# Attention and two dense layers on one core: transposes that write tokens in order, the softmax guard on ScalarE, low parts of weights on either engine, and a new issue order

## The chip, the core and the metric

The kernel runs on one NeuronCore of a Trainium2 chip. The metric is device time in microseconds (us): 627.39 us, the median of three runs (627.38 to 627.73). TensorE (PE) multiplies matrices into PSUM banks; VectorE (DVE), ScalarE (ACT) and GpSimd (POOL) work on tiles; SyncE (SP) issues the DMAs. Each engine works off its own queue in order and waits on semaphores for the others.

## The reference

```python
def _attn_ref(q, k, v):                       # (2, 8, 768, 64) each
    k_sum = k.reshape(B, H, nb, 32, D).max(axis=3)
    v_sum = v.reshape(B, H, nb, 32, D).mean(axis=3)
    scores_l = scale * q @ k.T                # kept where |i - j| < 16
    scores_s = scale * q @ k_sum.T + np.log(32)
    scores_all = np.concatenate([scores_l_m, scores_s], axis=-1)
    a = np.exp(scores_all - max)
    a = a / (np.sum(a, axis=-1, keepdims=True) + 1e-09)
    return a @ np.concatenate([v, v_sum], axis=2)

x = attn_out.transpose(0, 2, 1, 3).reshape(1536, 512)
h = x @ w_in;  x = (h * np.clip(h + 3, 0, 6) / 6) @ w_out        # 512 -> 2048 -> 512
h = x @ w_in2; return (h * sigmoid(h)) @ w_out2                  # the same sizes
```

## The kernel before

The tokens of a batch are cut into 12 units of 64 queries, 24 units in all. A unit `u` sees 96 keys around it and 24 block keys, 120 slots for each of 4 pairs of heads. Its steps are `keys` (key window gathered, POOL or DVE), `scores` (PE), `masked` (DVE: add the mask, take the maximum), `exps` (ACT: exponential with the row sum), `guard` (DVE: 1e-9 added to a 128x4 tile of sums), `inverse` (DVE), `normal` (POOL or DVE: 128x480 multiply), `turn` (PE transposes), `turned` (copy out of PSUM), `mix` (PE), `mixed_hi` and `mixed_lo` (the result as two fp32r parts, a high one and what is left).

Before that, `load` fetches two neighbouring tokens into one partition, `par` separates even from odd tokens, and `tr` transposes 128x128 pieces (four per call, 24 calls) into a PSUM bank: even tokens fill one 128-column stretch, odd ones the next. `k_copy`, `k_max` and `q_copy` put the tokens back in order as they read the bank. `q_copy` fills, for each pair of heads, the two diagonal blocks of the query tile (64 partitions each, one instruction for each, 48 instructions in all).

The dense layers take every product as high x high + high x low + low x high. A half weight `h` (64 of them, 128x1024 words of 32 bits holding 512 wide numbers) is fetched and converted: `conv_mag` (ACT), `conv_low`, `conv_clamp`, `conv_join`, `conv_sign` (DVE), `conv_hi` (ACT, or DVE where starred), `conv_lo` (GpSimd). Step `i` then has `hidden` (PE, 12 products), `act` (ACT), `gate` (DVE), `gate_hi`, `gate_lo`, `project` (PE, 12 products). The first 32 steps work on 256 tokens, the other 80 on 512. The first `hidden` needs the four first units' `mixed_lo`, and its weights.

The order of everything is the text `ORDER`, a list of 1920 steps; each engine's queue is that list with the other engines' steps left out. A star puts a step on DVE where its function asks for it (`copier`, `keys`, `normal`, `gate_lo`, `q_copy`). `conv_lo` does not ask: the 31 stars on it do nothing, and all 64 run on GpSimd. Buffers come from rings: 7, later 8 PSUM banks, 3 buffers of fetched words, 2 of `bits`, 1 of `mag`, 3 of gated results.

The lines that the text names: L481 par, L495 tr, L503 k_copy, L510 k_max, L526 and L528 q_copy on DVE and ACT, L535 v_pair, L573 v_put, L589 and L590 keys, L612 masked, L626 exps, L637 guard, L641 inverse, L646 normal, L654 turn, L659 turned, L666 mix, L688 and L692 mixed_hi and mixed_lo, L406 conv_mag, L411 conv_low, L418 conv_clamp, L424 conv_join, L431 conv_sign, L442 conv_hi, L445 conv_lo, L708 hidden, L728 and L732 gate, L736 gate_hi, L742 gate_lo, L764 and L767 project.

Of the kernel before, what the change touches and what calls it, by code (L numbers as in the profile page):

```python
# [87 lines left out]
k_max 0 2 0, keys 3*, keys 2*, tr q 0 1 0, k_copy 0 2 1, scores 3, q_copy 0 1 1 1, k_copy 0 2 0*, keys 1,
load v 0 0, conv_low 0, q_copy 0 1 1 0, keys 0, masked 3, conv_mag 0, scores 1, scores 2, conv_clamp 0,
conv_low 1, scores 0, conv_join 0, rouse 5, v_sums 0 0, masked 2, q_copy 0 1 0 0, keys 7, keys 4,  # L90
load q 0 2, masked 0, exps 3, keys 6, q_copy 0 1 0 1, tr q 0 2 0, tr q 0 2 1, conv_mag 1, conv_clamp 1,
guard 3, fetch 2, exps 2, rouse 0, inverse 3, keys 5, masked 1, scores 6, normal 3, exps 0, guard 2, turn 3,
inverse 2, conv_join 1, scores 7, conv_sign 0, conv_hi 0*, exps 1, load v 0 2, conv_mag 2, load v 0 1,
rouse 7, conv_sign 1, guard 0, conv_lo 0*, keys 10, inverse 0, rouse 3, rouse 4, q_copy 0 2 0 0, normal 2,
masked 7, rouse 2, q_copy 0 2 1 1, v_add 0 0, v_sums 0 2, v_sums 0 1, conv_hi 1, guard 1, scores 5,
conv_clamp 2, q_copy 0 2 1 0, turn 2, conv_low 2, fetch 3, load v 1 0, warm 0, normal 0, exps 7, v_add 0 1,
inverse 1, load_v 2, load_v 1, warm 1, q_copy 0 2 0 1, v_add 0 2, rouse 1, normal 1*, turn 1, load_v 3,
v_rows 0, turn 0, conv_join 2, masked 6, fetch 4, conv_mag 3, guard 7, conv_lo 1, turned 3, load_v 0,
turned 2, conv_sign 2, conv_low 3, masked 5, v_pair 1 0, turned 1, v_put 0 2, inverse 7, keys 9*, exps 5,
scores 4, load v 1 1, v_sums 1 0, conv_clamp 3, keys 8*, warm 2, conv_join 3, normal 7, guard 5, mix 2,  # L100
inverse 5, scores 9, v_put 0 0, mixed_hi 2, v_put 0 1, v_put 0 3, masked 4, conv_hi 2, unstage, normal 5,
conv_sign 3, mix 1, v_add 1 0, turned 0*, turn 5, load k 1 0, scores 8, conv_lo 2, exps 4, mixed_hi 1,
load_v 5, mixed_lo 2, v_pair 1 1, guard 4, mixed_lo 1, conv_hi 3, conv_mag 4, mix 3, inverse 4, turned 5,
mix 0, v_sums 1 1, turn 7, tr k 1 0 0, mixed_hi 0, mixed_hi 3*, conv_low 4, conv_clamp 4, conv_join 4,
keys 11, mixed_lo 0, exps 6, fetch 5, mixed_lo 3, turned 7, tr k 1 0 1, masked 9, guard 6, conv_lo 3,
fetch 6, inverse 6, load_v 4, conv_low 5, mix 5, conv_sign 4, hidden 1 0, normal 4, v_add 1 1, conv_mag 5,
k_max 1 0 1, exps 9, hidden 0 0, hidden 1 1, load k 1 1, conv_clamp 5, guard 9, conv_hi 4, conv_join 5,
hidden 0 1, act 0, turn 4, load_v 6, turned 4, inverse 9, fetch 7, mixed_hi 5, conv_mag 6, normal 6,
load_v 7, masked 8, gate 0, scores 10, mixed_lo 5, act 1, conv_lo 4, gate 1, conv_low 6, conv_clamp 6,
mix 4, scores 11, k_copy 1 0 1, conv_join 6, conv_sign 6, mixed_hi 4, gate_hi 0, turn 6, k_copy 1 0 0,  # L110
turned 6, hidden 2 0, tr k 1 1 1, tr k 1 1 0, conv_sign 5, conv_hi 6, k_copy 1 1 0, mixed_lo 4, gate_hi 1,
masked 10, mix 6, k_max 1 0 0, conv_lo 6, gate_lo 0, hidden 2 1, load k 1 2, mixed_hi 6, conv_low 7,
load v 1 2, conv_hi 5, fetch 8, mix 7, hidden 3 0, gate_lo 1, load_v 11, mixed_hi 7, conv_mag 7, fetch 9,
mixed_lo 7, k_max 1 1 0, k_copy 1 1 1, hidden 3 1, project 0 0, act 2, act 3, tr k 1 2 0, mixed_lo 6,
masked 11, gate 2, hidden 4 0, conv_lo 5, project 1 0, gate_hi 2, v_pair 1 2, gate 3, exps 10, conv_clamp 7,
hidden 4 1, conv_join 7, conv_low 8, k_max 1 1 1, gate_lo 2, k_copy 1 2 0, conv_sign 7, conv_mag 8,
# [828 lines left out]
```

## Time and profile before

| what | value |
|---|---|
| median of three runs | 627.39 us |
| the profiled execution's own time | 628.69 us |
| its span, first to last instruction | 626.9 us |
| PE busy | 605.1 us (97%) |
| DVE / ACT / POOL busy | 411.0 / 250.4 / 137.5 us |
| mean granted TensorE clock | 0.997 |

The profiled execution took 1.3 us more than the median of the runs; 1.8 us of it lie outside the span. PE's 97% leaves 21.8 us idle. Where they lie is read from a table by stage, below: most of them are in the first 47 us, in which the attention's first units and the first weights are made ready by DVE, ACT and POOL, and the first `hidden` starts at 47.76 us.

### The profile page before, as it was taken

What the parts mean: (1) busy time and instruction counts of PE and PEld (TensorE: products, weight loads), DVE (VectorE), ACT (ScalarE), POOL (GpSimd) and SP (SyncE); (2) the same over time, 40 slices, a digit from 0 to 9 for tenths busy, and PEclk for the clock granted to TensorE, in tenths of its full rate; (3) what the DMA queues carried; (4) which work ended last, traced back from release to release, by engine and by line L of the source; (5) the groups of instructions that cost most, each with busy time, mean ns of one, the idle gap of its engine ahead of it and who ended that gap; (6) DMA issues with size and microseconds to landing.
All of it is one profiled execution on the core that took longest, in us unless ns stands there. A gap on an engine that the chain in (4) does not pass through costs nothing.

```text
span 626.9 us, 9556 instructions
## 1 busy us (share of the span) xinstructions
PE 605.1 (97%) x3590; PEld 518.8 (83%) x3590; DVE 411.0 (66%) x920; ACT 250.4 (40%) x603; POOL 137.5 (22%) x131
## 2 busy tenths in 40 slices
...
GB/s 252 266 226 191 182 173 145 15 51 11 64 58 101 100 102 67 101 122 47 67 68 35 100 101 67 68 67 68 2 66 34 43 25 2 0 68 1 67 1 67
DMA packets 69054, 51.61 MB, mean 82 GB/s; under 512 B 36368, under 2 KB 63504, under 8 KB 69008
## 3 DMA queue, kind: packets, MB, share of 16 engines
...
q14 instruction: 18, 0.15, 0.1%
...
## 4 chain that ended last, share of the span: by engine, by line
PE 76%; DVE 17%; ACT 3%; issue 2%; DMA 1%; POOL 0%; SPq 0%; ACTq 0%; DVEq 0%; POOLq 0%
PE bank L708 35%; PE bank L767 20%; PE bank L764 16%; DVE bits L424 2%; DVE bits L431 2%; DVE bits L411 2%; DVE mag L418 2%; PE bank L597 1%; PE bank L666 1%; DVE gw L742 1%; DVE stat L637 1%; DVE prob L612 1%; PE bank L654 1%; DMA stage<-in_k_dram 1%; PE bank L495 1%
## 5 line engine op out<-in xcount | busy, mean ns | idle before, releaser
L708 PE MATMUL bank<-x,w 128*128 128x512 f32 (+1 forms) x912 | 185.0, 349 | 1.1 <-DVE rn L728 1.0
L708 PEld LDWEIGHTS bank<-x,w 128*128 128x128 f32 x912 | 149.0, 191 | 23.5 <-DVE rn L728 2.0
L445 POOL TENSOR_TENSOR w<-bits,w 128x512 fp32r<-128x512 f32 x48 | 70.5, 1473 | 241.6 <-ACT w L442 139.9
L767 PE MATMUL bank<-w,gw 128*128 128x512 f32 (+1 forms) x456 | 103.6, 378 | 0.1
L767 PEld LDWEIGHTS bank<-w,gw 128*128 128x128 f32 x456 | 82.5, 188 | 16.6 <-DVE gw L742 0.5
L722 ACT ACTIVATE rw<-bank 128x512 f32<-128x512 f32 x48 | 28.3, 597 | 131.9 <-PE bank L708 98.6
L742 DVE TENSOR_TENSOR gw<-rw,gw 128x512 fp32r<-128x512 f32 x80 | 59.4, 749 | 32.0 <-ACT gw L736 30.3
L732 DVE TENSOR_TENSOR rw<-bank,rw 128x512 f32<-128x512 f32 x48 | 32.8, 687 | 63.3 <-ACT rw L722 63.0
L708 PE MATMUL bank<-x,we 128*128 128x512 f32 x240 | 59.3, 389 | 0.0
L764 PE MATMUL bank<-gw,w 128*128 128x512 f32 x240 | 58.6, 390 | 0.3 <-DVE gw L742 0.3
L406 ACT ACTIVATE mag<-words 128x512 f32<-128x512 f32 x64 | 43.1, 673 | 36.4 <-DVE bits L424 28.0
L764 PE MATMUL bank<-gn,w 128*128 128x256 f32 x384 | 54.6, 287 | 1.0 <-DVE gn L742 0.5
L764 PEld LDWEIGHTS bank<-gw,w 128*128 128x128 f32 x240 | 44.9, 188 | 10.4 <-DVE gw L742 1.2
L708 PEld LDWEIGHTS bank<-x,we 128*128 128x128 f32 x240 | 45.0, 188 | 9.4
L431 DVE SCALAR_TENSOR_TENSOR bits<-words,bits 128x512 uint32<-128x512 uint32 x64 | 50.7, 795 | 0.6
L736 ACT CAST gw<-rw 128x512 fp32r<-128x512 f32 x43 | 26.7, 621 | 60.2 <-PE bank L767 26.7
L764 PEld LDWEIGHTS bank<-gn,w 128*128 128x128 f32 x384 | 48.7, 191 | 2.0 <-issue 0.8
L424 DVE SCALAR_TENSOR_TENSOR bits<-mag,bits 128x512 uint32<-128x512 uint32 x64 | 49.4, 772 | 1.1
L411 DVE TENSOR_SCALAR bits<-words 128x512 uint32<-128x512 uint32 x64 | 36.7, 573 | 9.2 <-POOL w L445 5.7
L418 DVE TENSOR_SCALAR mag<-mag 128x512 f32<-128x512 f32 x64 | 33.9, 529 | 8.7 <-ACT mag L406 8.5
L445 POOL TENSOR_TENSOR we<-bits,we 128x512 fp32r<-128x512 f32 x16 | 22.2, 1393 | 75.7 <-DVE we L442 45.4
L736 DVE CAST gw<-rw 128x512 fp32r<-128x512 f32 x37 | 16.5, 449 | 33.6 <-PE bank L767 29.4
(105 smaller groups left out, 764.6 us busy)
## 6 DMA issues: line engine op xcount, KB each, us to landing
...
```

The costliest lines, as they stand in the source:

```text
L406: nc.scalar.activation(out=out, in_=low_high(h)[:, 1].bitcast(F32), func=AF.Abs, scale=EXP_SHIFT)
L411: nc.vector.tensor_scalar(out=bitss.take(h, 2), in0=low_high(h)[:, 0], scalar1=2.0**-29, scalar2=7.0, op0=ALU.mult, op1=ALU.min,)
L418: nc.vector.tensor_scalar(out=mag, in0=mag, scalar1=MAG_MIN, scalar2=MAG_MAX, op0=ALU.max, op1=ALU.min)
L424: nc.vector.scalar_tensor_tensor(out=bits, in0=mags.use(h).bitcast(U32), scalar=3, in1=bits, op0=ALU.logical_shift_left, op1=ALU.bitwise_or,)
L431: nc.vector.scalar_tensor_tensor(out=bits, in0=low_high(h)[:, 1], scalar=0x80000000, in1=bits, op0=ALU.bitwise_and, op1=ALU.bitwise_or,)
L445: nc.gpsimd.tensor_tensor(out=w_half(h, 1), in0=bitss.use(h).bitcast(F32), in1=w_half(h, 0).bitcast(F32), op=ALU.subtract,)
L708: nc.tensor.matmul(ps[:, :n], w[:, a, kk * P : (kk + 1) * P], x[:, o // SUB : (o + n) // SUB, b, kk, :], start=(m == 0), stop=(m == last),)
L732: nc.vector.tensor_tensor(out=r[:, :n], in0=ps[:, :n], in1=r[:, :n], op=ALU.mult)
L736: copier("gate_hi", i)(out=gs.take(i, 1)[:, 0, :n], in_=rs.use(i)[:, :n])
L742: eng.tensor_tensor(out=g[:, 1, :n], in0=r[:, :n], in1=g[:, 0, :n].bitcast(F32), op=ALU.subtract)
L764: nc.tensor.matmul(ps[:, o : o + n], lhs, g[:, b, :n], **flags)
L767: nc.tensor.matmul(ps[:, : len(cols)], g[:, a, rows], rhs, **flags)
```

## The change

Five edits are made together. (1) `tr` writes even tokens to even columns and odd ones to odd columns of the bank, so a transpose's output has a stride of two elements, and the readers (`k_copy`, `k_max`, `q_copy`, `mixed`) take tokens in order. (2) `q_copy` works on one head parity `e` for two pairs of heads: one instruction of 64x512 where two of 64x256 stood; 24 instead of 48. (3) `guard` becomes an ACT instruction. (4) `conv_lo` goes to DVE where starred: 37 of 64, 7 of them before the attention's buffers are given up. (5) `ORDER` is another permutation of the same 1920 steps, with other stars.

```diff
 ORDER = """
-table 0, load k 0 1, par k 1 1, load q 0 0, par k 1 0, tr k 0 1 1, par q 0 0, load k 0 0, par q 0 1,
...
+zero, table 0, load k 0 0, par k 0 1, par k 0 0, tr k 0 0 1, tr k 0 0 0, rouse 7, k_max 0 0 1, load k 0 2,
...
@@ -442,7 +441,8 @@
         copier("conv_hi", h)(out=w_half(h, 0), in_=bitss.use(h).bitcast(F32))
 
     def conv_lo(h):
-        nc.gpsimd.tensor_tensor(
+        eng = nc.vector if ("conv_lo", h) in ON_DVE else nc.gpsimd
+        eng.tensor_tensor(
             out=w_half(h, 1), in0=bitss.use(h).bitcast(F32), in1=w_half(h, 0).bitcast(F32),
             op=ALU.subtract,
         )
@@ -488,12 +488,12 @@
         key = (what, b, T)
         raw = raws.use(key) if key in raws.held else parts.use((what + "p", b, T))
         ps = banks.take((what, b, T, half), 2)
+        tokens = ps.rearrange("p (i j r) -> p i r j", i=2, r=2)
         for i in range(2):
             h0 = 2 * (2 * half + i)
             for r in range(2):
-                o = (2 * i + r) * P
                 nc.tensor.transpose(
-                    ps[:, o : o + P], raw[:, r * DM + h0 * D : r * DM + h0 * D + P], ident
+                    tokens[:, i, r], raw[:, r * DM + h0 * D : r * DM + h0 * D + P], ident
                 )
 
     def k_copy(b, T, half):
@@ -501,31 +501,31 @@
         hs = slice(2 * half, 2 * half + 2)
         dst = kT[b][:, hs, PAD + 256 * T : PAD + 256 * (T + 1)]
         copier("k_copy", b, T, half)(
-            out=dst.rearrange("p i (j r) -> p i r j", r=2),
-            in_=ps.rearrange("p (i r j) -> p i r j", i=2, r=2),
+            out=dst, in_=ps.rearrange("p (i t) -> p i t", i=2)
         )
 
     def k_max(b, T, half):
         ps = banks.use(("k", b, T, half))
         nc.vector.tensor_reduce(
             out=kmax[b][:, 2 * half : 2 * half + 2, 8 * T : 8 * (T + 1)],
-            in_=ps.rearrange("p (i r n j) -> p i n r j", i=2, r=2, n=8),
-            axis=AX.XY,
+            in_=ps.rearrange("p (i n t) -> p i n t", i=2, n=8),
+            axis=AX.X,
             op=ALU.max,
         )
 
-    def q_copy(b, T, half, i):
+    def q_copy(b, T, half, e):
         if (b, T) not in qTs.held:
             qTs.take((b, T), 4)
         ps = banks.use(("q", b, T, half))
-        dst = qTs.see((b, T))[:, 2 * half + i].rearrange("p w (e r j) -> p w e r j", e=2, r=2)
-        src = ps[:, 256 * i : 256 * (i + 1)].rearrange("p (r w j) -> p w r j", r=2, w=4)
-        for e in range(2):
-            rows = slice(e * D, e * D + D)
-            if ("q_copy", b, T, half, i) in ON_DVE:
-                nc.vector.tensor_scalar_mul(dst[rows, :, e], src[rows], 1.0 / math.sqrt(D))
-            else:
-                nc.scalar.mul(dst[rows, :, e], src[rows], 1.0 / math.sqrt(D))
+        rows = slice(e * D, e * D + D)
+        dst = qTs.see((b, T))[rows, 2 * half : 2 * half + 2, :, e * QW : e * QW + QW].rearrange(
+            "p i w t -> p (i w) t"
+        )
+        src = ps[rows].rearrange("p (v t) -> p v t", t=QW)
+        if ("q_copy", b, T, half, e) in ON_DVE:
+            nc.vector.tensor_scalar_mul(dst, src, 1.0 / math.sqrt(D))
+        else:
+            nc.scalar.mul(dst, src, 1.0 / math.sqrt(D))
 
     def v_pair(b, T):
 
@@ -634,7 +634,7 @@
 
     def guard(u):
         st = sts.see(u)
-        nc.vector.tensor_scalar_add(st[:, 1], st[:, 1], 1e-9)
+        nc.scalar.activation(out=st[:, 1], in_=st[:, 1], func=AF.Identity, bias=1e-9)
 
     def inverse(u):
         st = sts.use(u)
@@ -674,11 +674,8 @@
     def mixed(u):
         ps = banks.use(("m", u))
         j, o = divmod(u * QW, WIDE)
-        src = ps[:, : NHP * QW].rearrange("p (h r j) -> p h r j", h=NHP, r=2)
-        hi, lo = (
-            x1[j][:, o // SUB, i, :, o % SUB : o % SUB + QW].rearrange("p h (j r) -> p h r j", r=2)
-            for i in range(2)
-        )
+        src = ps[:, : NHP * QW].rearrange("p (h q) -> p h q", h=NHP)
+        hi, lo = (x1[j][:, o // SUB, i, :, o % SUB : o % SUB + QW] for i in range(2))
         return src, hi, lo
 
     def mixed_hi(u):
@@ -842,7 +839,7 @@
     raws = ring(apool, "qkv", 2, [P, 2 * DM])
     gs = ring(apool, "gn", LAG + 1, [P, 2, SUB], F32R)
     rs = ring(apool, "rn", 2, [P, SUB])
-    qTs = ring(apool, "qT", 2, [P, NHP, 4, P])
+    qTs = ring(apool, "qT", 2, [P, NHP, 4, 2 * QW])
     sts = ring(apool, "stat", 4, [P, 3, NHP])
```

Line numbers differ between the two kernels: in the changed one `guard` is still L637, but `hidden` is L705 (L708 before), `mixed_lo` L689 (L692), `mixed_hi` L685 (L688), `conv_join` L423 (L424), `conv_sign` L430 (L431), `conv_clamp` L417 (L418), `conv_low` L410 (L411), `conv_mag` L405 (L406), `conv_hi` L441 (L442), `k_max` L509 (L510).

On DVE, this is what stands before, around the `mixed_lo` (L692) of the first four units, whose results the first `hidden` waits for (`x_0` is the tile of the first tokens, `stat` a unit's sums, `bits` and `mag` weights in conversion):

```order
L555 COPY vsum<-bank_80 128x128
L659 COPY pT_111<-bank_76 120x512
L692 TENSOR_TENSOR x_0_64<-bank_78,x_0_64 128x4x2x32
L637 TENSOR_SCALAR stat_105<-stat_105 128x4
L692 TENSOR_TENSOR x_0_64<-bank_77,x_0_64 128x4x2x32
L641 RECIPROCAL stat_105<-stat_105 128x4
L688 CAST x_0_64<-bank_81 128x4x2x32
L411 TENSOR_SCALAR bits_69<-words_72 128x512
L418 TENSOR_SCALAR mag_68<-mag_68 128x512
L424 SCALAR_TENSOR_TENSOR bits_69<-mag_68,bits_69 128x512
L692 TENSOR_TENSOR x_0_64<-bank_80,x_0_64 128x4x2x32
L692 TENSOR_TENSOR x_0_64<-bank_81,x_0_64 128x4x2x32
```

And on DVE now, at the same place (the `mixed_lo` are L689; L573 is `v_put`, L535 `v_pair`, L445 `conv_lo`):

```order
L423 SCALAR_TENSOR_TENSOR bits_70<-mag_68,bits_70 128x512
L573 COPY early_units<-bank_75 24x512
L430 SCALAR_TENSOR_TENSOR bits_70<-words_72,bits_70 128x512
L689 TENSOR_TENSOR x_0_64<-bank_81,x_0_64 128x4x64
L535 TENSOR_TENSOR qkv_93<-qkv_93 128x8x64
L689 TENSOR_TENSOR x_0_64<-bank_78,x_0_64 128x4x64
L689 TENSOR_TENSOR x_0_64<-bank_79,x_0_64 128x4x64
L689 TENSOR_TENSOR x_0_64<-bank_76,x_0_64 128x4x64
L445 TENSOR_TENSOR w_91<-bits_69,w_91 128x512
L641 RECIPROCAL stat_103<-stat_103 128x4
L417 TENSOR_SCALAR mag_68<-mag_68 128x512
```

No `guard` stands there any more; a `v_put`, a `v_pair` and a `conv_lo` that ran on ACT and POOL do.

On ACT, the first `exps` (L626) and what stands between them before (L528 is `q_copy`, L406 `conv_mag`):

```order
L626 ACTIVATE early_units,stat_102<-early_units,stat_102 128x120 x4
L528 ACTIVATE qT_101<-bank_77 64x4x64 x2
L406 ACTIVATE mag_68<-words_72 128x512
L626 ACTIVATE early_units,stat_103<-early_units,stat_103 128x120 x4
L626 ACTIVATE prob_109,stat_104<-prob_109,stat_104 128x120 x4
L626 ACTIVATE prob_110,stat_105<-prob_110,stat_105 128x120 x4
```

And on ACT now, from the first `exps` on (L637 is `guard`, L441 `conv_hi`):

```order
L626 ACTIVATE early_units,stat_102<-early_units,stat_102 128x120 x4
L637 ACTIVATE stat_102<-stat_102 128x4
L405 ACTIVATE mag_68<-words_73 128x512
L626 ACTIVATE early_units,stat_103<-early_units,stat_103 128x120 x4
L637 ACTIVATE stat_103<-stat_103 128x4
L626 ACTIVATE prob_109,stat_104<-prob_109,stat_104 128x120 x4
L441 CAST w_90<-bits_70 128x512
L637 ACTIVATE stat_104<-stat_104 128x4
L626 ACTIVATE prob_110,stat_105<-prob_110,stat_105 128x120 x4
```

Each unit's `guard` follows its `exps` on the same engine, once with a `conv_hi` between them.

On PE, the first `hidden` (L708) and what precedes it before (L544 is `v_sums`, L654 `turn`, L495 `tr`, L666 `mix`):

```order
L544 MATMUL bank_76<-qkv_94,cst 32x128 x4
L654 MATMUL bank_78<-cst,early_units 120x128 x4
L495 MATMUL bank_77<-cst,qkv_93 128x128 x4
L495 MATMUL bank_74<-cst,qkv_93 128x128 x4
L666 MATMUL bank_80<-pT_112,vwin_114 64x64 x8
L708 MATMUL bank_81<-x_0_64,w_91 128x256 x6
L708 MATMUL bank_78<-x_0_64,w_90 128x256 x6
```

And on PE now (L597 is `scores`, L705 `hidden`):

```order
L666 MATMUL bank_78<-pT_112,vwin_114 64x64 x8
L666 MATMUL bank_76<-early_units 64x64 x8
L654 MATMUL bank_75<-cst,prob_109 120x128 x4
L597 MATMUL bank_81<-kw_107,qT_100 128x120 x4
L654 MATMUL bank_78<-cst,early_units 120x128 x4
L705 MATMUL bank_79<-x_0_64,w_90 128x256 x6
L544 MATMUL bank_76<-qkv_94,cst 32x128 x4
L705 MATMUL bank_75<-x_0_64,w_91 128x256 x6
```

In both queues about the same attention work stands ahead of the first `hidden`: ten `scores`, six `turn`, five `mix` and fourteen `tr` before, twelve, six, four and twelve now.

## Rows read from the trace of the kernel before

**Rows 1.** Table by stage; engine columns are busy us (instructions), then PE's granted clock.
```profile
0.00:47.20 47.20, 31.27 (x326) 26.56 (x328) 38.19 (x132) 38.34 (x117) 24.99 (x39) 1.00 1.04 248
47.20:80.00 32.80, 32.28 (x300) 30.69 (x295) 32.53 (x90) 24.20 (x73) 14.79 (x12) 0.95 0.71 177
80.00:120.00 40.00, 38.18 (x363) 35.84 (x362) 34.17 (x100) 26.92 (x81) 16.85 (x18) 1.00 0.51 130
200.00:300.00 100.00, 99.85 (x440) 82.09 (x439) 80.36 (x132) 39.46 (x69) 23.42 (x18) 1.00 0.30 95
600.00:627.00 27.00, 23.76 (x128) 20.35 (x126) 10.73 (x19) 1.80 (x3) 0.00 (x0) 1.00 0.11 39
```

**Rows 2.** Timeline around the first `hidden`: start us, duration us, engine; idle before it in brackets.
```profile
46.93 0.90 PE L666 MATMUL bank<-pT,vwin 120*64 120x64 f32 x16 [2.49 <-DVE x L692]
...
47.76 4.40 PE L708 MATMUL bank<-x,w 128*128 128x256 f32 x24
```

**Rows 3.** The guard in that timeline, free and beside a POOL instruction.
```profile
47.93 0.16 DVE L637 TENSOR_SCALAR stat<-stat 128x4 f32<-128x4 f32 x1
...
48.23 0.42 DVE L411 TENSOR_SCALAR bits<-words 128x512 uint32<-128x512 uint32 x1
...
50.76 1.55 POOL L445 TENSOR_TENSOR w<-bits,w 128x512 fp32r<-128x512 f32 x1 [1.28 <-ACT w L442]
51.08 1.25 DVE L637 TENSOR_SCALAR stat<-stat 128x4 f32<-128x4 f32 x1
```

**Rows 4.** DVE groups, 0 to 47.2 us: count, busy us, mean ns, idle before.
```profile
L411 DVE TENSOR_SCALAR bits<-words 128x512 uint32<-128x512 uint32 x5 | 4.0, 792 | 0.0
L418 DVE TENSOR_SCALAR mag<-mag 128x512 f32<-128x512 f32 x5 | 3.8, 755 | 0.2 <-ACT mag L406 0.2
L637 DVE TENSOR_SCALAR stat<-stat 128x4 f32<-128x4 f32 x7 | 3.7, 532 | 0.6 <-ACT prob L626 0.6
L526 DVE TENSOR_SCALAR qT<-bank 64x256 f32<-64x256 f32 x2 | 0.8, 418 | 0.0
L503 DVE COPY kT<-bank 128x512 f32<-128x512 f32 x1 | 0.7, 680 | 0.0
L589 DVE COPY kw<-kT 128x384 f32<-128x384 f32 x2 | 0.7, 334 | 0.0
L590 DVE COPY kw<-kmax 128x96 f32<-128x96 f32 x2 | 0.4, 197 | 0.0
```

**Rows 5.** POOL groups, 0 to 47.2 us.
```profile
L445 POOL TENSOR_TENSOR w<-bits,w 128x512 fp32r<-128x512 f32 x4 | 5.7, 1414 | 2.7 <-DVE w L442 2.0 <-ACT w L442 0.7
L646 POOL TENSOR_TENSOR prob<-prob,stat 128x480 f32<-128x480 f32 x3 | 3.4, 1129 | 1.7 <-ACT x L688 1.7
L646 POOL TENSOR_TENSOR early_units<-early_units,stat 128x480 f32<-128x480 f32 x3 | 3.0, 1003 | 3.8 <-DVE stat L641 3.8
L535 POOL TENSOR_TENSOR qkv<-qkv 128x512 f32<-128x512 f32 x2 | 2.7, 1351 | 0.2 <-DMA qkv<-in_v_dram 0.2
```

**Rows 6.** ACT groups over the whole run.
```profile
L720 ACT ACTIVATE rw<-bank 128x512 f32<-128x512 f32 x32 | 18.8, 595 | 39.7 <-PE bank L708 19.8 <-DVE gw L742 19.8
L528 ACT ACTIVATE qT<-bank 64x256 f32<-64x256 f32 x42 | 15.8, 377 | 1.6 <-PE bank L495 0.6 <-DVE qT L526 0.5
L626 ACT ACTIVATION_READ_ACCUMULATOR prob<-prob,stat 128x1 f32 x72 | 13.6, 189 | 0.0
```

**Rows 7.** DVE, a subtraction of the size of `conv_lo`, whole run; then the guard, 0 to 120 us.
```profile
L742 DVE TENSOR_TENSOR gw<-rw,gw 128x512 fp32r<-128x512 f32 x80 | 59.4, 749 | 32.0 <-ACT gw L736 30.3
...
L637 DVE TENSOR_SCALAR stat<-stat 128x4 f32<-128x4 f32 x16 | 8.5, 532 | 0.9 <-ACT prob L626 0.9
```

**Rows 8.** Timeline, 90 to 92 us: a DVE instruction that reads two SBUF tiles.
```profile
90.85 1.15 POOL L646 TENSOR_TENSOR early_units<-early_units,stat 128x480 f32<-128x480 f32 x1
91.08 1.20 DVE L742 TENSOR_TENSOR gn<-rn,gn 128x256 fp32r<-128x256 f32 x1
```

**Rows 9.** PE, the transposes L495 of loaded tiles, whole run.
```profile
L495 PE MATMUL bank<-cst,qkv 128*128 128x128 f32 x64 | 9.5, 275 | 1.5 <-DMA qkv<-in_q_dram 1.5
```

More of the change, by code (lines that the diff above doesn't have):

```diff
@@ L88 @@
[L88 to L116, printed above, removed]
-normal 9, conv_hi 7, act 4, v_sums 1 2, v_add 1 2, exps 11, conv_clamp 8, conv_join 8, conv_sign 8,
@@ L133 @@
-project 9 0, conv_sign 13, mixed_hi 8, q_copy 1 0 0 0, conv_clamp 14, v_put 1 0, conv_join 14, mixed_lo 8,
-project 9 1, load q 1 1, gate 10, gate_hi 10, conv_sign 14, hidden 13 0, gate_lo 10*, scores 13, conv_hi 14,
-inverse 10, normal 11, conv_lo 14, masked 13, hidden 13 1, fetch 18, act 13, gate 13, keys 15, conv_mag 15,
-scores 12, hidden 11 0, conv_low 15, load q 1 2, masked 12, gate_lo 12, turn 11, conv_hi 13, v_put 1 1,
-gate_hi 13*, hidden 11 1, conv_lo 13*, normal 10*, exps 13, gate_lo 13, act 11, conv_clamp 15, guard 13,
@@ L143 @@
-gate_hi 15, mix 10, tr q 1 1 1, fetch 16, keys 17*, scores 14, turn 12, project 13 0, mixed_hi 10*,
-project 13 1, turned 12, masked 14, inverse 15, q_copy 1 1 1 1, tr q 1 2 0, gate_lo 14, mix 13, mixed_lo 10,
-normal 15*, q_copy 1 2 0 0, exps 14, q_copy 1 1 1 0, project 14 0, q_copy 1 2 0 1*, gate_lo 15*,
-hidden 18 0, guard 14, project 14 1, project 15 0, tr q 1 2 1, inverse 14, turn 15, hidden 18 1,
-finish 0 0 0 0, act 18, scores 17, normal 14, gate 18, turned 15, project 15 1, turn 14, keys 16*,
@@ new lines @@
+q_copy 0 2 0 1, conv_low 3, conv_join 3, guard 7, inverse 7, normal 7, scores 9, load_v 0, fetch 4, guard 4,
+v_put 0 3, load_v 3, masked 5, turned 1, conv_mag 4, conv_sign 3, conv_clamp 4, inverse 4, normal 4,
+conv_low 4, scores 11, mix 3, v_put 0 1, scores 10, v_put 0 0, mix 0, masked 6, conv_join 4, exps 5,
+guard 5, turned 2, mixed_hi 0, mixed_hi 3, load_v 1, mix 1, load_v 2, v_put 0 2*, conv_sign 4, mixed_hi 1,
+conv_hi 4, mixed_lo 0, load v 1 1, v_pair 1 1*, mixed_lo 1, mixed_lo 3, conv_hi 3, mix 2, mixed_hi 2,
```

404 lines of the change are left out of this document (219 added, 185 removed).

## The prediction, made before the changed kernel ran

> **What bounds the kernel now.** I read the table by stage first. PE is busy 200 of 200 us in the middle and, from 47.2 us to 120, idle only 32.8-32.28 + 40-38.18 = 2.3 us; in the first 47.2 us it is idle 15.9, and 3.2 us in the last slice, where the last results leave [rows 1]. So the time is PE's work, which no edit shortens, plus those waits. PE's wait before the first products of the dense layers is the one to look at: the `mix` at 46.93 us had waited 2.49 us for DVE's `mixed_lo`, and the first `hidden` follows at 47.76 [rows 2]. DVE is busy 38.2 of these 47.2 us; 5.8 of the rest is the first DMA. ACT has 38.3, its table load included, but DVE is what PE waits for [rows 1, 2]. So the start is DVE's queue up to the fourth `mixed_lo`: what is in it, and how long its instructions are held up.
>
> They are held up. The guard takes 0.16 us at 47.93, yet 1.25 us at 51.08, when a POOL subtraction runs from 50.76 to 52.31; `conv_low` (L411) takes 0.42 us alone [rows 3] and 0.79 on average up to 47.2 us, `conv_clamp` (L418), of the same kind and size, 0.755 [rows 4]. Guards: 7 x (0.53-0.16) = 2.6 us lost. The two conversions: 5 x (0.79-0.42) + 5 x (0.755-0.42) = 3.5 us. The POOL work beside it is 12 large instructions, 14.8 us [rows 5].
>
> **The change, part by part.** *DVE up to the fourth `mixed_lo`.* By the two queues, out go 7 guards, 3.7 us [rows 4], and three small ones, a reciprocal, a `v_add`, a `mixed_hi`, which I put at 0.2, 0.3 and 0.4 us, about the sizes of the smaller rows there (a 128x96 copy 0.2, 64x256 from PSUM 0.42 [rows 4]). In come three `keys` pairs at 0.33+0.20 [rows 4], 1.6 us; one `conv_sign`, one `turned` and one `v_put`, each a 512-wide instruction, at the 0.68 of the 512-wide copy [rows 4], 2.0 us; one `v_pair` at 0.75 [rows 7]; and two `q_copy` of 64x512 where two of 64x256 stood. The trace has no 64x512; it lies between 0.42 and 0.68, and as the width and not the partitions sets the others, I take 0.68: +0.5. In: 4.9 us; out: 4.6. Net +0.3.
>
> *What holds DVE up.* POOL has in its queue, up to the same place, 3 `conv_lo` and 5 `normal`, no `v_pair`: 8 large instructions for 12. If the 3.5 us of the conversions fall in proportion, 3.5 x 8/12 = 2.3: -1.2. The other stretched instructions (joins, signs, copies) I leave. The bounds: if the stalls do not fall at all, 0; and a guard's stall may pass on to the instruction behind it, up to the whole 2.6 us. If instead they all but vanish, -3.5. I take -1.2, the proportional share. The first `hidden` comes 0.3 - 1.2 = -0.9 us earlier.
>
> The start-up itself stays: the first DVE instruction still waits for the first load of k. The query tile now comes fourth in SP's queue, but `scores` need the maxima of all of k anyhow. The mask table is issued behind one more fetch of weights (512 KB; at the 248 GB/s of that stage [rows 1], 2 us later). It is wanted by the first `masked`, which the new order puts behind seven more DVE instructions, so I take 0; without that cover it would cost up to 2 us.
>
> *ACT.* Seven guards come in. The nearest small ACT instruction takes 0.19 us, the next one up 0.38 (64x256) [rows 6]: 1.3 us, at most 2.7. The `q_copy` go from 22 x 0.377 = 8.3 us to 10 x 0.595 = 6.0, taking the 512-wide ACT row [rows 6]. ACT is 1.0 us lighter, between 2.3 lighter and 0.4 heavier. The guard now runs behind its own `exps` with no change of engine, and DVE no longer stands in its queue waiting for it (0.6 us [rows 4]): -0.6.
>
> *Copies and transposes.* On DVE `k_max`, `mixed_hi` and `mixed_lo` read as many elements as before; 0, with the gain of a plain order unknown (0 to -0.5 us in all, as none is much above its like). The 96 transposes write with a stride of two. The trace has none such; 64 of them took 0.148 us each [rows 9]. At one end nothing changes; at the other each takes twice that, 96 x 0.148 = 14 us, of which a third lies in PE's idle time. I take 0, as the number of columns is the same.
>
> *From 47 to 120 us.* Nine guards leave DVE, 8.5-3.7 = 4.8 us [rows 4, 7]; seven `conv_lo` come, 7 x 0.75 = 5.2 us [rows 7], and leave POOL, 7 x 1.41 = 9.9 us of its 31.6 here [rows 1, 5]. With a third of POOL's work gone, DVE is held up less. PE can gain no more than its 2.3 us of idle and the 0.05 x 32.8 = 1.6 us that the granted clock of 0.95 costs [rows 1]. I take -0.5, between -3 and +2.
>
> *After 120 us.* Thirty more `conv_lo` put 22.5 us on DVE, which is busy 80 of 100 us at most there [rows 1], while PE waits 0.15 us in that stretch. I take 0 and keep +1: a `gate` queued behind a `conv_lo` is 0.75 us later, while a step is 24 products of PE.
>
> Sum: -0.9 - 0.6 - 0.5 = -2.0 us. The profiled execution took 628.7 us (a span of 626.9 and 1.8 around it), so it would be 626.7; it stood 1.3 above the median of 627.4, and on that scale the forecast is **625.4 us**, its own range 623.0 to 626.1.
>
> **The rivals.** *A: the stalls only move.* A guard that waits 1.1 us for POOL is gone, but the next DVE instruction that meets the same POOL instruction waits in its place: the 2.6 us come back, and -2.0 becomes +0.6: 628.0 us, within what a measurement of this kernel can tell from no change (0.2%, 1.25 us). For it: the subtraction L742 took 1.20 us beside a POOL multiply [rows 8], against a mean of 0.75 for one twice as wide [rows 7], so `conv_lo` and `v_pair`, which read two tiles as it does, can be held up as the guard was. Against it: the instructions that follow a guard in these queues are often `masked` and `mixed_lo`, which read PSUM. The Trainium skill (SBUF — State Buffer, Who interferes with whom) says that a DVE instruction with two SBUF inputs contends with a GpSimd instruction that reads SBUF, and that the one issued second waits until the first ends; by that rule moving `conv_lo` to DVE does not leave the contest, it enters it from the other side. The rows just named agree.
>
> *B: slower, DVE late at the first `hidden`.* The place is the same queue. If the shorter POOL list frees nothing and the guards' 2.6 us pass on in full, and DVE waits as often as before, it is 0.3 + 2.6 = +2.9 there, and with nothing won afterwards 630.3 us. It decides once DVE needs over 38.2 + 1.25 = 39.4 us of work up to the fourth `mixed_lo`. For it: net of stalls the new queue is longer. Against: 8 POOL instructions instead of 12.
>
> *C: more is won.* ACT lighter and POOL lighter end cross-waits too: the conversions' 3.5 us go entirely instead of by 1.2, and 1 us more of the later idle: -2.0 - 2.3 - 1.0 = -5.3, 622.1 us. Against: DVE's list is not shorter.
>
> *D: the strided transposes cost.* Two thirds of the 14 us bound: 636 us. Nothing speaks for it but that no row shows such a write.
>
> **How the numbers follow.** Forecast 0.42, C 0.08, A 0.28, B 0.19, D 0.03. Faster by over 0.2% 0.50, within 0.2% 0.28, slower 0.22. The range reaches to C's price below and short of B's above: 622.3 to 629.5 us.
>
> **What would show it.** The first `hidden` at 45.5 to 47.3 us; DVE busy at most 37.7 us up to it; `conv_low` and `conv_clamp` at a mean under 0.7 us there; no DVE row for the guard, and an ACT row of about 0.2 us; PE idle under 2.3 us from there to 120 us, and still under 1 us in 200 to 400. It is wrong if the first `hidden` is no earlier than 47.8 us, if `conv_clamp` and the joins are stretched as much as before (A or B), or if the transposes' mean is above 0.15 us (D).

## The result and the profile after

The changed kernel took 619.94 us (median of 4 runs, 619.72 to 620.51) against 627.43 (627.38 to 627.73): a ratio of 0.9881, 95% interval 0.9864 to 0.9898, or 7.5 us less. The forecast of 625.4 us had the right sign, but the result lies 2.4 us below the range that it gave (622.3 to 629.5). The profiled execution took 620.01 us, a span of 618.2, against 628.69 and 626.9; that of before stood 1.3 us above its median, so the traces differ by 8.7 us where the medians differ by 7.5.

The stage table of the changed kernel (stretch and its length in us; busy us and instructions of PE, weight loads, DVE, ACT and POOL; granted clock, DMA share, GB/s), to be laid beside [rows 1]:

```profile
0.00:47.20 47.20, 35.23 (x329) 32.02 (x330) 36.94 (x143) 35.67 (x109) 20.55 (x32) 0.96 0.93 231
47.20:80.00 32.80, 32.80 (x338) 31.17 (x337) 31.17 (x88) 25.42 (x83) 17.81 (x17) 1.00 0.99 229
80.00:120.00 40.00, 40.00 (x397) 38.49 (x396) 31.49 (x103) 27.15 (x84) 9.71 (x14) 1.00 0.38 99
200.00:300.00 100.00, 100.00 (x443) 82.76 (x442) 77.63 (x137) 36.36 (x64) 9.33 (x6) 1.00 0.29 92
600.00:619.00 19.00, 15.09 (x81) 12.88 (x79) 7.48 (x13) 1.11 (x2) 0.00 (x0) 1.00 0.15 55
```

PE's idle time fell from 15.9 to 12.0 us in the first stage and from 2.3 us to nothing between 47.2 and 120 us. In that second stretch (the two rows added) PE did 735 instructions where it had done 663. POOL was busy 27.5 us there for 31.6, and DVE 62.7 for 66.7, though DVE had been given the work. Further on PE's pace is the same: 443 instructions in 100 us for 440.

All that PE still waits for, by the list of its waits (who waited for whom: us in total, times, longest):

```profile
PE bank L495 <- DVE stage L481: 6.8, 2, 5.9
PE bank L563 <- DVE vsum L557: 2.1, 1, 2.1
PE bank L597 <- ACT qT L528: 1.7, 1, 1.7
PE bank L654 <- POOL prob L646: 1.2, 1, 1.2
```

The first is the start-up; the wait for `mixed_lo` of [rows 2] is not in the list any more. The timeline at that place (start, duration, engine):

```profile
44.28 1.08 DVE L689 TENSOR_TENSOR x<-bank,x 128x256 fp32r<-128x256 f32 x3
...
45.23 1.07 PE L705 MATMUL bank<-x,w 128*128 128x256 f32 x6
```

The first `hidden` starts at 45.23 us for 47.76, right behind the fourth `mixed_lo`. From there to the end of the span it is 573.0 us, for 579.1 before. So in these two traces a third of the 8.7 us lies ahead of that point and two thirds behind it. The share ahead is uncertain: a second trace of the old program up to there (the kernel with only the late low parts changed, below) has its first `hidden` at 46.04 us, which would leave 0.8 us ahead and 5.0 behind. The chain of work that ended last, followed back from the last instruction, tells it by engine, as shares of the span. Before and now:

```profile
PE 76%; DVE 17%; ACT 3%; issue 2%; DMA 1%; POOL 0%; SPq 0%; ACTq 0%; DVEq 0%; POOLq 0%
PE 95%; DVE 3%; DMA 1%; issue 0%; ACT 0%; SPq 0%; DVEq 0%; ACTq 0%
```

DVE was on that chain for 17% of the span and is now for 3%.

DVE's groups in the first 47.2 us (count, busy us, mean ns, idle before), which answer to [rows 4]:

```profile
L417 DVE TENSOR_SCALAR mag<-mag 128x512 f32<-128x512 f32 x6 | 2.7, 458 | 0.2 <-ACT mag L405 0.2
L410 DVE TENSOR_SCALAR bits<-words 128x512 uint32<-128x512 uint32 x6 | 2.5, 412 | 0.0
...
L526 DVE TENSOR_SCALAR qT<-bank 64x512 f32<-64x512 f32 x2 | 1.3, 673 | 0.0
...
L445 DVE TENSOR_TENSOR w<-bits,w 128x512 fp32r<-128x512 f32 x1 | 0.7, 682 | 0.0
```

`conv_low` is at 0.41 us, the time it takes alone, where it had been 0.79; `conv_clamp` at 0.46 for 0.755. POOL in the same stretch, answering to [rows 5]:

```profile
L445 POOL TENSOR_TENSOR w<-bits,w 128x512 fp32r<-128x512 f32 x4 | 5.8, 1458 | 3.9 <-DVE w L441 3.9
L646 POOL TENSOR_TENSOR prob<-prob,stat 128x480 f32<-128x480 f32 x4 | 4.4, 1098 | 8.1 <-DVE stat L641 8.1
L646 POOL TENSOR_TENSOR early_units<-early_units,stat 128x480 f32<-128x480 f32 x2 | 2.0, 996 | 5.5 <-DVE stat L641 5.5
L535 POOL TENSOR_TENSOR qkv<-qkv 128x512 f32<-128x512 f32 x1 | 1.3, 1272 | 0.0
```

Eleven large POOL instructions for twelve; nine of them start ahead of the fourth `mixed_lo`, where the forecast counted eight (it missed the `v_pair`, which ran on POOL at 41.49 us). So the conversions' stall did not go in proportion to POOL's work: of the ten `conv_low` and `conv_clamp` up to there, nine start while none of these nine runs. Over the whole run, the guard on ACT, the wider `q_copy` and the transposes [rows 6, 9]:

```profile
L528 ACT ACTIVATE qT<-bank 64x512 f32<-64x512 f32 x17 | 10.0, 590 | 1.2 <-PE bank L495 0.9
...
L637 ACT ACTIVATE stat<-stat 128x4 f32<-128x4 f32 x24 | 4.8, 204 | 0.4
```

```profile
L495 PE MATMUL bank<-cst,qkv 128*128 128x128 f32 x64 | 9.6, 277 | 0.0
```

The guard takes 0.204 us (0.19 was taken for it) and the copy 0.590 (0.595 taken); a transpose with a stride of two takes 0.150 us for 0.148.

### The profile page after: what moved, and what is told of

The parts are those of the page before. It is cut to its first block, busy times and chain, and to the rows that moved or that the text cites. A ratio compares the mean times of both kernels' runs of the same rounds, so it can differ in the third digit from the quotient of the medians.

```text
span 618.2 us, 9465 instructions
## 1 busy us (share of the span) xinstructions
PE 603.1 (98%) x3590; PEld 521.0 (84%) x3590; DVE 402.4 (65%) x934; ACT 244.1 (39%) x596; POOL 87.8 (14%) x100
## 4 chain that ended last, share of the span: by engine, by line
PE 95%; DVE 3%; DMA 1%; issue 0%; ACT 0%; SPq 0%; DVEq 0%; ACTq 0%
PE bank L705 43%; PE bank L761 22%; PE bank L764 21%; PE bank L597 3%; PE bank L666 2%; PE bank L495 2%; PE bank L654 2%; DMA stage<-in_k_dram 1%; DVE early_units L612 0%; DVE prob L612 0%; PE bank L563 0%; DVE early_units L590 0%; ACT qT L528 0%; DVE kmax L509 0%; PE bank L875 0%
## 5 line engine op out<-in xcount | busy, mean ns | idle before, releaser
L705 PE MATMUL bank<-x,w 128*128 128x512 f32 (+1 forms) x912 | 180.5, 347 | 0.0
L705 PEld LDWEIGHTS bank<-x,w 128*128 128x128 f32 x912 | 147.1, 189 | 21.0 <-issue 0.4
L739 DVE TENSOR_TENSOR gw<-rw,gw 128x512 fp32r<-128x512 f32 x80 | 56.0, 705 | 32.2 <-ACT gw L733 30.1
L445 POOL TENSOR_TENSOR w<-bits,w 128x512 fp32r<-128x512 f32 x23 | 32.5, 1413 | 284.8 <-ACT w L441 173.3
L705 PE MATMUL bank<-x,we 128*128 128x512 f32 x240 | 58.6, 390 | 0.0
L405 ACT ACTIVATE mag<-words 128x512 f32<-128x512 f32 x64 | 43.0, 671 | 35.9 <-DMA words<-in_moe_w_in_dram 15.7
L705 PEld LDWEIGHTS bank<-x,we 128*128 128x128 f32 x240 | 45.1, 188 | 9.3
L430 DVE SCALAR_TENSOR_TENSOR bits<-words,bits 128x512 uint32<-128x512 uint32 x64 | 45.7, 717 | 0.8
L423 DVE SCALAR_TENSOR_TENSOR bits<-mag,bits 128x512 uint32<-128x512 uint32 x64 | 45.2, 706 | 1.5
L417 DVE TENSOR_SCALAR mag<-mag 128x512 f32<-128x512 f32 x64 | 29.7, 463 | 12.5 <-ACT mag L405 12.0
L410 DVE TENSOR_SCALAR bits<-words 128x512 uint32<-128x512 uint32 x64 | 29.0, 453 | 11.6 <-DMA words<-in_moe_w_in_dram 5.0
L764 PE MATMUL bank<-we,gw 128*128 128x512 f32 x144 | 34.8, 390 | 0.0
L761 PE MATMUL bank<-gw,we 128*128 128x512 f32 x144 | 34.8, 389 | 0.0
```

The costliest lines, as they stand in the source:

```text
L405: nc.scalar.activation(out=out, in_=low_high(h)[:, 1].bitcast(F32), func=AF.Abs, scale=EXP_SHIFT)
L410: nc.vector.tensor_scalar(out=bitss.take(h, 2), in0=low_high(h)[:, 0], scalar1=2.0**-29, scalar2=7.0, op0=ALU.mult, op1=ALU.min,)
L417: nc.vector.tensor_scalar(out=mag, in0=mag, scalar1=MAG_MIN, scalar2=MAG_MAX, op0=ALU.max, op1=ALU.min)
L423: nc.vector.scalar_tensor_tensor(out=bits, in0=mags.use(h).bitcast(U32), scalar=3, in1=bits, op0=ALU.logical_shift_left, op1=ALU.bitwise_or,)
L430: nc.vector.scalar_tensor_tensor(out=bits, in0=low_high(h)[:, 1], scalar=0x80000000, in1=bits, op0=ALU.bitwise_and, op1=ALU.bitwise_or,)
L445: eng.tensor_tensor(out=w_half(h, 1), in0=bitss.use(h).bitcast(F32), in1=w_half(h, 0).bitcast(F32), op=ALU.subtract,)
```

## The experiments

Every time is given as a ratio to the kernel before, run beside it on the same chip, and as the difference from 1 times 627.4 us. The theories named below are those of the expectation quoted ahead of each result. DVE's four conversions (`conv_low`, `conv_clamp`, `conv_join`, `conv_sign`, 16 each) and 16 guards took 54.6 us together up to 120 us in the kernel before (12.9 + 12.4 + 11.5 + 9.3 + 8.5); this sum is called the five groups below. Its four conversions, the guard being in [rows 7]:

```profile
L431 DVE SCALAR_TENSOR_TENSOR bits<-words,bits 128x512 uint32<-128x512 uint32 x16 | 12.9, 814 | 0.2
L424 DVE SCALAR_TENSOR_TENSOR bits<-mag,bits 128x512 uint32<-128x512 uint32 x16 | 12.4, 777 | 0.2
L411 DVE TENSOR_SCALAR bits<-words 128x512 uint32<-128x512 uint32 x16 | 11.5, 718 | 0.0
L418 DVE TENSOR_SCALAR mag<-mag 128x512 f32<-128x512 f32 x16 | 9.3, 580 | 0.3 <-ACT mag L406 0.2
```

A single trace scatters: the kernel with only the late low parts changed runs the old program up to 120 us, and its trace gives 53.8 us for the five groups there.

**Code and order apart.** First the changed code with the old order. That order already carried stars on 31 `conv_lo`, which the old code ignores; seven lie ahead of 120 us.

```diff
 ORDER = """
-zero, table 0, load k 0 0, par k 0 1, par k 0 0, tr k 0 0 1,
...
+table 0, load k 0 1, par k 1 1, load q 0 0, par k 1 0, tr k 0 1 1,
...
```

> The changed functions (order of tokens, one query copy per parity, guard on ScalarE, low parts on VectorE where starred) under the issue order and stars of the kernel before. Theory W (the work taken off VectorE and its stalls beside GpSimd make the gain, whatever the order): 621 to 624 us, the first hidden product before 46.5 us. Theory O (the new order makes the gain, the edits of the functions matter little): 626 to 628 us, the first hidden product at 47 us or later.

Measured 0.9911 (0.9897 to 0.9926): -5.6 us, as theory W had it, with the first `hidden` at 45.19 us. Then the old code with the new order (the same diff the other way round, in the old kernel):

> The functions of the kernel before (guard on VectorE, all low parts on GpSimd, two query copies, tokens put in order by the readers) under the new issue order and stars. Theory W: 625 to 628 us, with guards of up to 1.2 us in VectorE's rows again. Theory O: 620 to 622 us, PE never idle after the first hidden product.

Measured 1.0216 (1.0191 to 1.0242): +13.6 us, far above both theories. PE's list of waits has two rows there that neither the kernel before nor the changed one has:

```profile
PE bank L597 <- POOL kw L590: 4.5, 2, 2.8
PE bank L597 <- DVE kw L590: 2.4, 1, 2.4
```

The new order puts `keys` (L590) behind work that the old code leaves on POOL and DVE; the first of the two rows comes back with the same numbers when only the low parts return to POOL (below). So the code is worth 5.6 us by itself; the order is worth about 2 us on top of it (0.9881 for 0.9911, whose intervals just meet), and costs 13.6 without it.

**One edit at a time, in the old kernel.** The guard on ACT:

```diff
-        nc.vector.tensor_scalar_add(st[:, 1], st[:, 1], 1e-9)
+        nc.scalar.activation(out=st[:, 1], in_=st[:, 1], func=AF.Identity, bias=1e-9)
```

> The kernel before, its order and all else, with only the guard moved to ScalarE. Theory G (the guard's stalls and its waits for ScalarE are the larger part of the 5.6 us that the edited functions won under the old order): 623 to 625 us, the first hidden product 1.5 to 3 us before 47.8 us. Rival A of the prediction (the next VectorE instruction inherits the stall): 626.5 to 628 us.

Measured 0.9968 (0.9958 to 0.9978): -2.0 us, 625.4 us, between the two theories. The five groups, four now, went from 54.6 to 47.4 us, 1.3 us more than without the 8.5 us of guards: of the guards' stall, 8.5 - 16 x 0.16 = 5.9 us, a fifth came back in the others, all of it in `conv_join` (0.777 to 0.880 us on average). Against the second trace of the old program (53.8 us, 8.7 of them guards) it is 2.3 us, two fifths. The timeline shows it at the very place of [rows 3]:

```profile
48.60 1.53 POOL L445 TENSOR_TENSOR w<-bits,w 128x512 fp32r<-128x512 f32 x1 [1.28 <-ACT w L442]
49.03 1.65 DVE L424 SCALAR_TENSOR_TENSOR bits<-mag,bits 128x512 uint32<-128x512 uint32 x1
```

In the kernel before the guard waited here, and L424 (`conv_join`), which came behind it, took 0.68 us. Now L424 meets the same POOL instruction and takes 1.65.

The low parts on DVE, where the old order's 31 stars say so:

```diff
-        nc.gpsimd.tensor_tensor(
+        eng = nc.vector if ("conv_lo", h) in ON_DVE else nc.gpsimd
+        eng.tensor_tensor(
```

> The kernel before with only the 31 low parts that carry a star moved to VectorE (7 of them before 190 us). Theory G: 626 to 628 us, they come too late for the first hidden product and cost VectorE as much as they relieve it. Rival P (fewer GpSimd instructions beside VectorE is the larger part): 622 to 625 us.

Measured 0.9919 (0.9901 to 0.9937): -5.1 us, the largest of the three and in rival P's range. Up to 120 us the five groups, and the new `conv_lo` (L446) last (line numbers as before, the guard's one further down):

```profile
L431 DVE SCALAR_TENSOR_TENSOR bits<-words,bits 128x512 uint32<-128x512 uint32 x16 | 14.0, 882 | 0.1
L424 DVE SCALAR_TENSOR_TENSOR bits<-mag,bits 128x512 uint32<-128x512 uint32 x16 | 11.4, 711 | 0.2
L411 DVE TENSOR_SCALAR bits<-words 128x512 uint32<-128x512 uint32 x16 | 10.4, 652 | 0.0
...
L418 DVE TENSOR_SCALAR mag<-mag 128x512 f32<-128x512 f32 x16 | 8.7, 542 | 0.2 <-ACT mag L406 0.2
...
L638 DVE TENSOR_SCALAR stat<-stat 128x4 f32<-128x4 f32 x16 | 6.3, 394 | 0.7 <-ACT prob L627 0.6
...
L446 DVE TENSOR_TENSOR w<-bits,w 128x512 fp32r<-128x512 f32 x7 | 4.9, 694 | 0.0
```

They are 50.8 us: 3.8 less (3.0 against the second trace), against 4.9 us of added `conv_lo`. Other DVE groups, among them `keys` and `normal`, were held up less as well, so that all of DVE's busy time up to 120 us fell, from 104.9 to 102.6 us. PE had done 1021 instructions at 120 us, for 978 (990 in the second trace).

The layout (the diff of `tr`, `k_copy`, `k_max`, `q_copy` and `mixed` shown ahead of the prediction, alone):

> The kernel before with only the transposes that write tokens in order and one query copy per head parity; guard on VectorE, low parts on GpSimd, old order. Theory G, ScalarE not being what PE waits for: 626.5 to 628 us, transposes as long as before (0.148 us). Rival S (ScalarE's 2 to 4 us matter): 623.5 to 625.5 us. Were a strided write slower: over 630 us.

Measured 0.9982 (0.9972 to 0.9991): -1.1 us, on theory G's side. Its first `hidden` came at 43.5 us, 2.5 to 4.2 us earlier (against the two traces of the old program), but from there to the end took 581.3 us, 2.2 more than before: much of what was won at the start was lost again, and PE was idle 3.8 us between 47.2 and 120 us for 2.3.

Alone the three give -8.2 us, together under the old order -5.6: they partly win the same waits.

**One edit taken back, in the changed kernel.** The guard back on DVE, which is the guard's diff reversed:

> The changed kernel with only the guard put back on VectorE, at its place in the new order. Theory W (guards and their stalls held VectorE up): 622 to 625 us, first hidden product 1.5 to 3 us later than 45.2 us. Theory O, or a stall that only moves from one VectorE instruction to the next: 619.5 to 620.8 us.

Measured 0.9988 (0.9978 to 0.9999): 6.7 us of the 7.5 are gone, more than either theory allowed; the first `hidden` came at 48.31 us. Up to 120 us DVE stood idle 7.0 us before the guards, waiting for `exps` on ACT:

```profile
L637 DVE TENSOR_SCALAR stat<-stat 128x4 f32<-128x4 f32 x16 | 5.8, 360 | 7.0 <-ACT early_units L626 3.6 <-ACT prob L626 3.4
```

All low parts back on POOL (the low parts' diff reversed):

> The changed kernel with all 64 low parts back on GpSimd, order and all else as changed. Theory W: the low parts beside VectorE stall it again, 621 to 623 us, with 0.5 to 2 us of PE idle between 45 and 120 us. Theory O: 619.5 to 620.8 us, since GpSimd has time left over and only 7 of the 37 lie before 170 us.

Measured 1.0037 (1.0023 to 1.0051): the whole gain is gone and 2.3 us more, above both theories. In the new order the low parts are worth 9.8 us. The row of `keys` is again in PE's list:

```profile
PE bank L596 <- POOL kw L589: 4.5, 2, 2.8
```

The old layout:

> The changed kernel with the old transposes, two query copies and readers that put tokens in order; guard on ScalarE, low parts where starred, new order. Theory G: 620 to 622 us, ScalarE only 2 to 4 us busier. Rival S, and a new order that leaves ScalarE no room: 623 to 626 us.

Measured 0.9903 (0.9882 to 0.9925): 1.4 us of the gain go, as theory G had it and about what the layout won alone. The intervals of this run and of the changed kernel overlap, so the sign is not certain.

**Why the low parts win.** Two halves of that edit, in the old kernel: only the seven ahead of 120 us, and only the 24 behind.

```diff
-        eng = nc.vector if ("conv_lo", h) in ON_DVE else nc.gpsimd
+        eng = nc.vector if h in (0, 8, 9, 10, 11, 13, 15) else nc.gpsimd
```

> The kernel before with only the seven low parts before 120 us (h = 0, 8, 9, 10, 11, 13, 15) on VectorE; the other 57 stay on GpSimd. If the prediction's step for 47 to 120 us is the one that was mis-sized, the whole gain of the 31 is here: 622.5 to 623.7 us (622.75 with all 31), since PE waits only 0.4 us behind 120 us in the kernel before. Rival: the later 24 count too, by giving VectorE and GpSimd a slack that a later stretch uses: 624.5 to 626.

> The complement: the 24 low parts behind 120 us on VectorE, the seven before it on GpSimd as before. If all of the gain is in the early seven: 626.7 to 627.6 us (PE's waits of 0.4 us in 200 to 400 us may go). If the later ones count: 625 to 626.3.

Measured 0.9947 (0.9932 to 0.9962), -3.3 us, and 0.9986 (0.9976 to 0.9996), -0.9 us. Two thirds of the 5.1 us are in the seven, ahead of 120 us; that all would be (622.5 to 623.7 us) was missed, and the 24 that the prediction put at nothing count about 0.9. The two halves give 4.2; what is left lies within the intervals. The gain of the seven lies behind the first `hidden`, which comes at 46.09 us with them and at 46.04 in the other half: PE's count of instructions stands at 990 at 116.5 us in the one and at 120 us in the other, 3.5 us later.

Then POOL got work back at the seven places, without the data. In each, `spare` is a scratch tile of 128x448 that DVE fills once at the start (0.43 us), `BESIDE` holds the seven, and the DVE `conv_lo` of the 31 stays. First a subtraction that reads:

```diff
+        if h in BESIDE:
+            nc.gpsimd.tensor_tensor(out=spare, in0=spare, in1=spare, op=ALU.subtract)
```

> The low parts' edit alone (622.75 us) with GpSimd given work again at the same seven places before 120 us: behind each of the conversions h = 0, 8, 9, 10, 11, 13 and 15 GpSimd subtracts a scratch tile of 128x448 from itself, two inputs read from SBUF, some 1.2 us each, waiting for nobody. Theory P1, that the gain came from VectorE no longer being held up by GpSimd's reads: VectorE's busy time before 120 us goes back up from 102.6 by 5 to 7 us to 108-110, and the time is 626 to 629 us. Theory P2, that it came from GpSimd's queue no longer standing behind conversions that wait for ScalarE: nothing waits here, VectorE stays at 103-104, the time is 622.5 to 624. Theory P3, that GpSimd's occupied time itself was what cost: the time is that of the run with memsets, 625 to 627, VectorE unchanged.

Measured 1.0007 (0.9997 to 1.0017): the whole gain is gone, as P1 had it, though DVE's busy time rose to 106.4 us and not to 108. Second, three fills that only write (`nc.gpsimd.memset(spare, 0.0)`):

> As the run with reads, but at the seven places GpSimd fills the scratch tile three times (some 0.4 us each, so again some 1.2 us of GpSimd), which writes and reads nothing. P1 (reads beside VectorE cost): VectorE's busy time before 120 us stays at 102.6-104 and the time at 622.5 to 624. P2 (waits in GpSimd's queue cost): the same 622.5 to 624. P3 (occupied GpSimd costs): 625 to 627, equal to the run with reads.

Measured 0.997 (0.9957 to 0.9983): -1.9 us, so 3.2 of the 5.1 are gone: P3's time, and not P1's, but less than with reads. Third, no work to speak of, but the wait for ACT in POOL's queue:

```diff
+        if h in BESIDE:
+            nc.gpsimd.tensor_copy(out=spare[:, 0:4], in_=w_half(h, 0)[:, 0:4].bitcast(F32))
```

> The low parts' edit alone (622.75 us), and at the seven places GpSimd copies four columns of the conversion's high part, which ScalarE has just written: some 0.1 us of work, but it stands in GpSimd's queue and waits for ScalarE as the whole conversion did before. P2 (the wait in GpSimd's queue was the cost): GpSimd's idle time before these copies is 8 us and more, the operations behind them come late as before, and the time goes back to 625.5 to 627.5 us. P1 (reads beside VectorE) and P3 (occupied GpSimd): the time stays at 622 to 623.5.

Measured 0.9915 (0.9901 to 0.993): the gain stays, though POOL waited as it was meant to. POOL's rows up to 120 us for these insertions, from the three traces in that order:

```profile
L453 POOL TENSOR_TENSOR spare<-spare 128x448 f32<-128x448 f32 x7 | 7.9, 1131 | 0.2
```

```profile
L454 POOL MEMSET spare<- 128x448 f32 x21 | 10.5, 501 | 0.9
```

```profile
L453 POOL COPY spare<-w 128x4 f32<-128x4 f32 x7 | 3.6, 521 | 14.0 <-ACT w L444 8.6 <-DVE w L444 5.3
```

Side by side, with DVE's share of the chain that ended last; up to 120 us the kernel with the late low parts alone is the kernel before once more:

| kernel | five groups, us | DVE busy to 120 us | DVE on the chain | PE instructions at 120 us | ratio |
|---|---|---|---|---|---|
| before | 54.6 | 104.9 | 17% | 978 | 1 |
| late low parts alone | 53.8 | 104.2 | 12% | 990 | 0.9986 |
| low parts (31) | 50.8 | 102.6 | 6% | 1021 | 0.9919 |
| + POOL waits | 50.3 | 103.2 | 5% | 1023 | 0.9915 |
| + POOL fills | 53.7 | 104.7 | 10% | 991 | 0.997 |
| + POOL reads | 54.1 | 106.4 | 12% | 970 | 1.0007 |

The wait in POOL's queue costs nothing that these runs show; POOL's work beside DVE does. The fills occupied POOL longer than the reads (10.5 against 7.9 us) and cost less, so the reads matter beyond the time that POOL is taken. `conv_lo` (L448 here), which reads two tiles, and `conv_low` and `conv_clamp` (L413, L420), which read one and a number and take 0.41 us alone, show the difference in the timeline. With reads:

```profile
69.63 3.71 POOL L453 TENSOR_TENSOR spare<-spare 128x448 f32<-128x448 f32 x3
...
71.40 1.15 DVE L413 TENSOR_SCALAR bits<-words 128x512 uint32<-128x512 uint32 x1
72.47 1.15 DVE L420 TENSOR_SCALAR mag<-mag 128x512 f32<-128x512 f32 x1
...
100.92 1.02 POOL L453 TENSOR_TENSOR spare<-spare 128x448 f32<-128x448 f32 x1
101.07 1.42 DVE L448 TENSOR_TENSOR w<-bits,w 128x512 fp32r<-128x512 f32 x1
```

and with fills:

```profile
69.14 5.03 POOL L454 MEMSET spare<- 128x448 f32 x9
...
70.93 0.54 DVE L413 TENSOR_SCALAR bits<-words 128x512 uint32<-128x512 uint32 x1
71.40 0.77 DVE L420 TENSOR_SCALAR mag<-mag 128x512 f32<-128x512 f32 x1
...
72.81 0.68 DVE L448 TENSOR_TENSOR w<-bits,w 128x512 fp32r<-128x512 f32 x1
```

Beside a read `conv_lo` took 1.42 us, beside fills its 0.68; the other two were held up by both, by 0.74 us beside reads and by 0.13 and 0.36 beside fills. The Trainium skill (SBUF — State Buffer, Who interferes with whom) says this: a DVE instruction with two SBUF inputs contends with a GpSimd instruction that reads SBUF, not with one that only writes it, while a `tensor_scalar` can enter a mode that contends with GpSimd through the shared pair of ports. These rows agree. A rival is that POOL's own work came later behind the inserted work. Up to 120 us no DVE instruction in these three traces waits for POOL, and PE's waits for POOL sum to 1.2 us with reads, 1.2 with fills and 1.1 with waits alone, so little of the loss reaches PE straight from POOL; how much comes round by other engines these runs don't separate.

**Further the same way.** The changed kernel with all 64 low parts on DVE (`eng = nc.vector`). The expectation speaks of 31 already there; the changed order has 37, so 27 more move.

> The changed kernel with all 64 low parts on VectorE instead of 31, so GpSimd has none; its new order was written for 31. VectorE gets 33 more of 0.69 us (22.8 us over the whole kernel, 6.2 before 120 us for nine of them), GpSimd loses 33 of 1.4. If each operation taken off GpSimd beside VectorE gives back a microsecond (P1), VectorE before 120 us falls from 99.6 to 96-98 and the time to 617 to 619.5. If the gain was that of GpSimd's queue (P2) or is used up, since PE waits for nobody after 34.5 us in the changed kernel: 619.5 to 621.5. Theory V, that VectorE becomes what PE waits for: 622 to 625.

Measured 0.9973 (0.996 to 0.9986): 5.8 us slower than the changed kernel, beyond even theory V's range (625.7 us). PE now waits for DVE:

```profile
PE bank L654 <- DVE stat L612: 2.6, 1, 2.6
PE bank L705 <- DVE w L445: 2.2, 3, 1.0
```

No version tried beats the changed kernel.

## Why the prediction was wrong, point by point

- *The step that failed is "From 47 to 120 us": -0.5 us.* It set 5.2 us of added `conv_lo` against 4.8 us of guards gone, and called POOL's relief "held up less" without pricing it. In the old kernel the seven `conv_lo` alone measure -3.3 us, all of it behind the first `hidden`, and all 31 -5.1. By the rows, the five groups lost 3.0 to 3.8 us for seven POOL instructions taken away, about 0.5 us for each. In the changed kernel PE's 2.3 us of idle time there went entirely, and the low clock left the stretch (0.95 to 1.00 up to 80 us), though for an earlier one. The bound of -3 in the text was about the value.
- *"What holds DVE up", -1.2 us, was mis-sized too.* The mechanism was right, the proportional share was not: up to 47.2 us the two conversions lost 3.5 us before; now `conv_clamp` loses 6 x (0.46 - 0.42) = 0.2 us and `conv_low` nothing. It is the bound of -3.5 that nearly came true, which was C's term. The new order did part of it: up to 120 us `conv_low` averages 0.718 us in the kernel before, 0.663 with the new code under the old order and 0.416 in the changed one. A count of POOL instructions doesn't tell which DVE instruction stands beside them. DVE was busy about 35.1 us up to the fourth `mixed_lo`, for 37.7 at most forecast.
- *First `hidden` 0.9 + 0.6 us earlier: it came 2.5 earlier.* That is by two single traces. Against the second trace of the old program (46.04 us) it is 0.8 us, less than forecast, so whether the start was under- or overrated stays open.
- *After 120 us: 0.* The late low parts are worth about 0.9 us (0.3 to 1.5); PE's 0.41 us of idle time in 200 to 400 us went.
- *The guard, -0.6 us on ACT's side.* Its price (0.204 us) was right. A's mechanism was shown, the stall that moved to L424, but with a fifth to two fifths of its size. The edit is worth 2.0 us alone, and 6.7 in the changed order, whose DVE queue would wait 7.0 us for `exps`.
- *Copies and transposes: 0.* Right for the transposes (D falls). The layout is worth 1.1 to 1.4 us; whether that comes from fewer `q_copy` or from readers that take tokens in order, no run separates.
- *B falls:* the first `hidden` was not late. *C*, at 0.08 and 622.1 us, came nearest, 2.2 us short: its conversions' 3.5 us went nearly whole. It was given a low chance because "DVE's list is not shorter", which counted work and not how long it is held up.
- *The sums.* The range of 622.3 us up does not reach C's 622.1, as it says it does. D's price, two thirds of 14.2 us, comes to 634.9 us on the forecast or 636.9 on the time before, and not to 636. The forecast's own range, 623.0 to 626.1, is narrower than the bounds of the step from 47 to 120 us alone (-3 to +2).
